# Attention followed by a feed-forward block on one Trainium2 core: Pool's arithmetic moved to DVE and ACT, and the two heads of a pair handled together

## The chip, the cores and the metric

The kernel runs on one core of a Trainium2 chip. A core has a matrix engine (PE, TensorE), a vector engine (DVE), a scalar engine for activations (ACT), a general engine (Pool, GpSimd) and a sync engine (SP) that here issues nearly all DMA transfers. Each has its own list of instructions, which in the traces of this case start in the order in which the program emits them (a copy on ACT at 411.43 us below, for one, starts behind three conversions emitted before it), and waits on the others by semaphores; that order matters more in this case than any single duration.

The metric is the time of one execution in microseconds (us). The kernel before scatters nonetheless, from 1007.5 to 1022.8 us over the chips used, so each kernel is compared with runs of the kernel before on the same chip in the same rounds. A ratio below is the mean time of one kernel's runs over that of the other's of the same rounds, so it is not quite the ratio of the medians that stand beside it; the brackets are its 95% interval.

## The reference, cut to what matters

```python
# attention: q, k, v of (4, 8, 768, 64); proj of (64, 6)
q_bits = (q @ proj > 0);  k_bits = (k @ proj > 0)        # 6 hash bits a row
mask   = q_bucket[..., :, None] == k_bucket[..., None, :]
scores = where(mask, q @ k.T / 8, -1e9)
attn   = exp(scores - max) / (sum + 1e-9)
x      = (attn @ v)  -> (3072, 512)
# feed-forward: w_in (512, 2048), w_out (2048, 512)
return relu(x @ w_in) ** 2 @ w_out
```

The arguments that `setup_inputs` makes for the weights are 64-bit floats (a 32-bit array times a NumPy double), so the kernel has to turn their bits into 32-bit floats itself.

## The kernel before

There are 32 heads, handled two at a time: 16 head pairs, `pr`, one head in each half of the 128 partitions. Each pair is cut into six key blocks (`SB` = 6), so there are 96 steps. A step computes scores of a key block (PE, to the tiles `st`), their exponentials (ACT, `e`), their running sum (DVE, `total`), and, two steps later, the product with the values (PE, `xo`). The masking is done by six hash bits (`bits`): they come from `near` and `far`, which PE computes from transposed inputs `feat`, which DVE transposes for the next pair at key blocks 2 (q) and 3 (k):

```python
PREPARE = ((), (), ((features, 0),), ((features, 1), (hash_bits, 0)), ((hash_bits, 1),), ())

def score(pr, kt):                      # before: one tile and one exponential per head
    ...                                 # matmuls into st[h, c]
    for c, (lo, hi) in enumerate(CUTS):         # columns 0:512 and 512:768
        for h in range(2):
            nc.scalar.activation(
                out=weights[pr, kt, h][:, lo:hi], in_=st[h, c][:, 0:hi - lo],
                func=ACTF.Exp, scale=scale,
            )
```

Between these, two 128x512 pieces of the weights per pair are converted from 64-bit to 32-bit floats: split into exponent and fraction bits on DVE (`part_weight`), the exponent clamped on Pool, and the fraction made a number on ACT; some steps later `round_weight` adds the low bits on DVE and multiplies by the power on Pool:

```python
def part_weight(i):                     # before
    nc.vector.tensor_scalar(out=power, in0=high, ...)     # exponent bits
    nc.vector.tensor_scalar(out=top, in0=high, ...)       # fraction bits
    nc.gpsimd.tensor_scalar(out=power, ..., op0=ALU.min, op1=ALU.max)
    nc.gpsimd.tensor_scalar(out=power, ..., op0=ALU.add, op1=ALU.mult)
    nc.scalar.activation(out=one, in_=top, func=ACTF.Copy, scale=2.0**-23, bias=1.0)

def round_weight(i):
    ...                                                   # two vector instructions
    nc.gpsimd.tensor_tensor(out=pieces[i][3], in0=one, in1=power.bitcast(FP32), op=ALU.mult)
```

The feed-forward stage multiplies by Strassen-like blocks (`product`), which need sums of blocks of its operands. Those of `w_in` (`sums_in`, eight groups of four additions) and of the first part of `x` (`sums_x`) are made during attention. `sums_in` writes over a block of `w_in`, so a copy of that block is stored to DRAM first (`kept_in`), and the first group has to wait until the store has read it:

```python
for u in range(len(steps) + 1):         # the order in which everything is emitted
    add_up(*steps[u - 1]); score(*steps[u])
    ...                                 # spread (reciprocals), PREPARE, attend, sum_up, normalize
    for f, i in w_steps.get(u, ()):     # the weight work of this step, and sums_in
        f(i)
    if u == W_IN:
        nc.sync.dma_start(out=kept_in, in_=w_in[:, 0:2, HF:DFF])
```

## Time and profile before

| | before |
|---|---|
| median of the first three runs | 1016.07 us (1013.56 to 1016.36) |
| span of the profiled run | 1018.9 us |
| one head pair, mean of 13 | 25.66 us |
| first feed-forward matmul | 424.92 us |
| a fixed point in the feed-forward stage (a group of its matmuls) to the end | 474.80 to 1018.90, 544.10 us |

The page's chain of work that ended last, by engine, and the group of the additions (line, engine, operation, output<-input, count | busy us, mean ns | idle before it and its cause) say the same thing from two sides:

```profile
PE 72%; DVE 13%; issue 7%; ACT 5%; DMA 1%; SPq 0%; ACTq 0%; DVEq 0%
L345 DVE TENSOR_TENSOR total<-total,e 128x768 f32<-128x768 f32 x128 | 145.6, 1180 | 3.0 <-ACT e L332 3.0
```

DVE carries 13% of the chain, far more than a helper of a PE-bound kernel should, and its additions take 1180 ns on average. The view of waits from 50 to 410 us (engine, tile and line, what it waited for: us in total, times, longest) sums what PE loses:

```profile
PE st L323 <- ACT e L332: 15.1, 14, 1.4
PE near L284 <- DVE feat L272: 14.4, 15, 3.0
PE near L284 <- ACT e L332: 12.7, 12, 1.3
```

About 42 us of waits in 14 pairs, three a pair.

### The profile page before, as it was taken

How to read it: one execution, taken by the hardware profiler on the slowest of the kernel's cores; microseconds unless marked ns; L12 is line 12 of the kernel's file. 1: busy time of each engine (PE TensorE's matmuls, PEld its weight loads, DVE VectorE, ACT ScalarE, POOL GpSimd, SP SyncE). 2: the span in 40 equal slices, each digit the busy share in tenths (PEclk: the TensorE clock that was granted, in tenths of full speed). 3: DMA queues.
4: the chain of work that ended last, by engine and by line, in shares of the span. 5: the costliest groups of instructions: out<-in, count | busy, mean ns of one | idle time of the engine just before them, and what ended most of it. 6: DMA issues, size and time to landing. Idle time of an engine off the chain costs nothing.

```text
span 1018.9 us, 13495 instructions
## 1 busy us (share of the span) xinstructions
PE 950.0 (93%) x5038; PEld 660.2 (65%) x5038; DVE 613.6 (60%) x1069; ACT 345.6 (34%) x817; POOL 218.0 (21%) x182
## 2 busy tenths in 40 slices
PE   6988989898888889999999999999999999999897
PEld 3333333333333333588888888888888888888786
DVE  1788888888988888998028604840583068106600
ACT  4655555555554555322013102310231032013200
POOL 1233424335776454590000000000000000000000
PEclk9999999999999999999999999999999999999999
DMA  7344444445533522101012202210221021100000
GB/s 165 90 100 113 104 108 105 108 102 148 136 86 92 139 70 85 37 0 43 21 52 67 69 21 68 63 57 21 83 63 52 21 88 58 52 21 1 1 21 23
DMA packets 121159, 70.14 MB, mean 69 GB/s; under 512 B 99328, under 2 KB 104448, under 8 KB 121088
## 3 DMA queue, kind: packets, MB, share of 16 engines
q1 hardware_dynamic: 121024, 69.22, 24.9%
q8 instruction: 41, 0.67, 0.3%
q14 instruction: 30, 0.25, 0.1%
q0 software_dynamic: 64, 0.00, 0.0%
HBM read 54.53 MB, written 14.68 MB: 68 GB/s over the span
## 4 chain that ended last, share of the span: by engine, by line
PE 72%; DVE 13%; issue 7%; ACT 5%; DMA 1%; SPq 0%; ACTq 0%; DVEq 0%
PE acc L554 54%; PE st L323 7%; PE xo L355 6%; ACT bits L290 3%; ACT e L332 3%; PE near L284 2%; DVE power L135 2%; DVE total L345 2%; DVE one L164 2%; DVE one L139 2%; DVE power L160 1%; DVE feat L272 1%; PE tot L372 1%; DVE g L645 1%; DVE h L644 1%
## 5 line engine op out<-in xcount | busy, mean ns | idle before, releaser
L332 ACT ACTIVATE e<-st 128x256 f32<-128x256 f32 (+1 forms) x384 | 157.0, 494 | 120.7 <-PE st L323 92.3
L554 PE MATMUL acc<-x,w_in 128*128 128x256 f32 x768 | 174.7, 379 | 0.0
L554 PE MATMUL acc<-w_out,g 128*128 128x256 f32 x768 | 170.0, 381 | 0.0
L554 PEld LDWEIGHTS acc<-w_out,g 128*128 128x128 f32 x768 | 146.9, 191 | 20.3
L554 PEld LDWEIGHTS acc<-x,w_in 128*128 128x128 f32 x768 | 145.8, 190 | 19.9
L323 PE MATMUL st<-feat,feat 64*128 64x512 f32 (+1 forms) x768 | 156.2, 492 | 0.0
L345 DVE TENSOR_TENSOR total<-total,e 128x768 f32<-128x768 f32 x128 | 145.6, 1180 | 3.0 <-ACT e L332 3.0
L355 PE MATMUL xo<-e,v_nat 128*64 128x512 f32 (+1 forms) x768 | 146.4, 501 | 0.8 <-ACT e L332 0.8
L554 PE MATMUL acc<-t_x,s_in 128*128 128x256 f32 x576 | 132.3, 379 | 2.7 <-ACT one L561 2.7
L554 PE MATMUL acc<-t_out,gs 128*128 128x256 f32 x576 | 126.3, 379 | 0.0
L554 PEld LDWEIGHTS acc<-t_x,s_in 128*128 128x128 f32 x576 | 109.2, 190 | 18.3 <-POOL w_out L431 1.9
L554 PEld LDWEIGHTS acc<-t_out,gs 128*128 128x128 f32 x576 | 109.4, 190 | 14.9
L355 PEld LDWEIGHTS xo<-e,v_nat 128*64 128x64 f32 x768 | 47.4, 137 | 92.2 <-issue 89.9
L677 DVE TENSOR_TENSOR o<-acc,two 128x256 f32<-128x256 f32 x12 | 5.1, 425 | 155.9 <-PE acc L554 155.9
L323 PEld LDWEIGHTS st<-feat,feat 64*128 64x128 f32 x768 | 69.3, 191 | 39.6 <-issue 37.5
L323 PE MATMUL st<-bits,bits 64*128 64x256 bf16 (+1 forms) x384 | 72.1, 330 | 21.1 <-ACT e L332 16.4
L645 DVE SCALAR_TENSOR_TENSOR g<-h 128x256 f32<-128x256 f32 x192 | 82.4, 450 | 5.0
L323 PEld LDWEIGHTS <-bits 64*128 64x128 bf16 x384 | 21.8, 94 | 82.0 <-issue 71.8
L561 ACT COPY two<-acc 128x256 f32<-128x256 f32 x60 | 22.4, 373 | 143.3 <-PE acc L554 143.3
L147 POOL TENSOR_SCALAR power<-power 128x512 uint32<-128x512 uint32 x32 | 54.2, 1694 | 2.6
L167 POOL TENSOR_TENSOR w_in<-one,power 128x512 f32<-128x512 f32 x16 | 34.1, 2130 | 83.3 <-DVE one L164 83.3
L284 PE MATMUL near<-feat,projs 64*64 64x384 f32 x120 | 26.5, 517 | 27.2 <-DVE feat L272 14.4
(90 smaller groups left out, 801.4 us busy)
## 6 DMA issues: line engine op xcount, KB each, us to landing
raw<-in_moe_w_in_dram SPq DMA_DIRECT2D x16, 512.0 KB, 4.3
raw<-in_moe_w_out_dram SPq DMA_DIRECT2D x16, 512.0 KB, 3.9
v_nat<-in_v_dram SPq DMA_DIRECT2D x16, 384.0 KB, 4.8
x_all<-x_t SPq DMA_DIRECT2D x16, 384.0 KB, 2.3
x<-x_all SPq DMA_DIRECT2D x6, 1024.0 KB, 5.3
out_dram<-o SPq DMA_DIRECT2D x24, 256.0 KB, 2.0
raw_qk<-in_k_dram SPq DMA_DIRECT2D x16, 384.0 KB, 3.2
raw_qk<-in_q_dram SPq DMA_DIRECT2D x16, 384.0 KB, 3.1
```

Source lines behind the costliest of these rows:

```text
L135: nc.vector.tensor_scalar(out=power, in0=high, scalar1=20, scalar2=0x7FF, op0=ALU.logical_shift_right, op1=ALU.bitwise_and,)
L147: nc.gpsimd.tensor_scalar(out=power, in0=power, scalar1=-896.0, scalar2=2.0**23, op0=ALU.add, op1=ALU.mult,)
L167: nc.gpsimd.tensor_tensor(out=pieces[i][3], in0=one, in1=power.bitcast(FP32), op=ALU.mult)
L284: nc.tensor.matmul(out=hp[at:at + D, 0:HS], lhsT=projs[rows], rhs=feat[pr, w][rows, c * HS:(c + 1) * HS], start=True, stop=True,)
L290: nc.scalar.activation(out=out, in_=in_, func=ACTF.Sign, scale=HUGE, bias=lifts[at])
L323: nc.tensor.matmul(out=st[h, c][:, 0:hi - lo], lhsT=src[pr, 1][rows, key], rhs=src[pr, 0][rows, lo:hi], start=first, stop=not first,)
L332: nc.scalar.activation(out=weights[pr, kt, h][:, lo:hi], in_=st[h, c][:, 0:hi - lo], func=ACTF.Exp, scale=scale,)
L345: nc.vector.tensor_tensor(out=totals[pr, h], in0=in0, in1=weights[pr, kt, h][:, 0:S], op=ALU.add)
L355: nc.tensor.matmul(out=xo[h * D:(h + 1) * D, lo:hi], lhsT=nat[pr, "v_nat"][:, h, kt * D:(kt + 1) * D], rhs=weights[pr, kt, h][:, lo:hi], s ...
L554: nc.tensor.matmul(out=acc[to], lhsT=a(i), rhs=b(i), start=first and i == 0, stop=last and i == n - 1, skip_group_check=True,)
L561: nc.scalar.copy(out=t, in_=acc[of])
L645: nc.vector.scalar_tensor_tensor(out=out, in0=h, scalar=0.0, in1=h, op0=ALU.max, op1=ALU.mult)
```

## The change

The intent: instructions of Pool slow those of DVE that run beside them (the numbers are in the prediction), so take all arithmetic off Pool while attention runs. The exponent's clamp becomes a Relu with an offset, written to 8 bits, whose range is meant to take the place of the upper limit; the final multiply and the block sums go to DVE. To make room, the exponentials and additions of both heads are merged (one tile `e` of 2 x 768 columns), and the last key block is not added by DVE: PE adds it with eight more matmuls against ones. The split of a weight piece moves from key block 4 to key blocks 5 (even pieces) and 0 of the next pair (odd ones). Cut to its core:

```diff
-        nc.gpsimd.tensor_scalar(... op0=ALU.min, op1=ALU.max)
-        nc.gpsimd.tensor_scalar(... op0=ALU.add, op1=ALU.mult)
+        nc.scalar.activation(out=small, in_=power, func=ACTF.Relu, bias=excess)     # uint8
+        nc.scalar.activation(out=power, in_=small, func=ACTF.Copy, scale=2.0**23)
         nc.scalar.activation(out=one, in_=top, func=ACTF.Copy, scale=2.0**-23, bias=1.0)
 ...
-        nc.gpsimd.tensor_tensor(
+        nc.vector.tensor_tensor(
             out=pieces[i][3], in0=one, in1=power.bitcast(FP32), op=ALU.mult
 ...
-        for c, (lo, hi) in enumerate(CUTS):
-            for h in range(2):
-                nc.scalar.activation(out=weights[pr, kt, h][:, lo:hi], in_=st[h, c]...)
+        for st, (lo, hi) in zip(sts, CUTS):
+            nc.scalar.activation(out=e[:, :, lo:hi], in_=st[:, :, 0:hi - lo], ...)
 ...
     def add_up(pr, kt):
+        if kt == 0 or kt == SB - 1:
+            return
 ...                                             # one addition for both heads
+        for src in (totals[pr], weights[pr, SB - 1]):        # sum_up, on PE
 ...
-        u = i // 2 * SB
-        for n, f in ((i % 2, load_weight), (4, part_weight), (SB + 1 + i % 2, round_weight)):
+        u = i // 2 * SB + i % 2
+        for n, f in ((-3, load_weight), (SB - 1, part_weight), (SB + 1, round_weight)):
 ...
-        w_steps.setdefault(W_IN + 4 * r + 1, []).append((sums_in, r))       # on Pool
+        w_steps.setdefault(W_IN + r * (SB - 1) + 1, []).append((sums_in, r)) # on DVE
```

## The prediction

> **What bounds the kernel now.** I read the page's header and slices first, then busy time by stage, then the idle gaps of PE, then one pair of heads on every engine.
>
> ```profile
> PE 950.0 (93%) x5038; PEld 660.2 (65%) x5038; DVE 613.6 (60%) x1069; ACT 345.6 (34%) x817; POOL 218.0 (21%) x182
> PE   6988989898888889999999999999999999999897
> DVE  1788888888988888998028604840583068106600
> POOL 1233424335776454590000000000000000000000
> ```
>
> Pool works only in the first 18 slices, up to about 460 us. Those are attention and the first part of the feed-forward stage, where PE has holes and DVE is nearly full. After that PE is solid. Busy time by stage (us: stretch and length, PE, PEld, DVE, ACT, POOL, then clock and DMA) puts sizes on it:
>
> ```profile
> 51.30:152.75 101.45, 89.15 (x585) 35.84 (x585) 85.01 (x109) 57.75 (x128) 37.19 (x24) 1.00 0.43 106
> 474.80:1018.90 544.10, 535.59 (x2475) 470.54 (x2474) 224.22 (x541) 97.67 (x262) 0.00 (x0) 1.00 0.14 45
> ```
>
> From 474.8 us on nothing that the change touches can matter: PE is the limit and its matmuls are unchanged. The attention stage lasts to 424.9 us (the first feed-forward matmul starts at 424.92). In the first row, exactly four head pairs, PE idles 12.3 us, 3.1 us a pair. The timeline of PE for one of them (start, length, what, idle before and releaser):
>
> ```profile
> 152.75 0.54 PE L284 MATMUL near<-feat,projs 64*64 64x384 f32 x2 [1.31 <-DVE feat L272]
> 157.72 0.54 PE L284 MATMUL near<-feat,projs 64*64 64x384 f32 x2 [0.93 <-ACT e L332]
> 164.12 0.86 PE L323 MATMUL st<-bits,bits 64*128 64x512 bf16 x2 [0.92 <-ACT e L332]
> ```
>
> Three waits a pair. The first two are hash matmuls waiting for a transpose that DVE makes late. For the second the view names ACT, but the k transpose ended at 157.57 (156.60 + 0.97) and the exponential is no input of this matmul, so I put it down to DVE. The third is ACT: exponentials stood behind a weight conversion, which stood behind DVE. Why DVE is late shows where its timeline is laid beside Pool's:
>
> ```profile
> 153.79 2.89 DVE L345 TENSOR_TENSOR total<-total,e 128x768 f32<-128x768 f32 x2
> 153.95 1.92 POOL L167 TENSOR_TENSOR w_in<-one,power 128x512 f32<-128x512 f32 x1 [2.96 <-DVE one L164]
> 157.50 1.78 DVE L345 TENSOR_TENSOR total<-total,e 128x768 f32<-128x768 f32 x2
> 162.96 0.63 ACT L150 ACTIVATE one<-one 128x512 f32<-128x512 uint32 x1 [0.74 <-DVE one L139]
> 163.50 1.61 ACT L332 ACTIVATE e<-st 128x512 f32<-128x512 f32 x4
> ```
>
> The same two additions take 1.78 us alone and 2.89 us beside a Pool multiply. The last two rows are the third wait: these exponentials read scores finished at 161.69 and start at 163.50. First feature matmul of pair 1 to that of pair 14 is 51.32 to 384.96 us, 333.64 / 13 = 25.66 us a pair.
>
> **What the Trainium skill says.** "SBUF — State Buffer", section "Who interferes with whom": a DVE instruction with two SBUF inputs contends with a GpSimd instruction that reads SBUF, and the later one waits. The trace agrees: 2.89 against 1.78 us. "VectorE: DVE Perf Modes", section "The perf-mode tier table (the rule you actually need)": fp32 tensor_tensor runs in 1x mode. Agreed: 0.89 us for 768 columns is above one per cycle at 0.96 GHz (0.80 us), so merging two additions saves almost nothing but the second's fixed cost. "ScalarE: Activation LUTs", section "What ACT_TABLE_LOAD costs": an ACTIVATE takes 186 ns + 0.833 ns a column, a pointer operand adds about 93 ns, and neighbours overlap by about 93 ns. The trace: 593 and 395 ns for 512 and 256 columns, where the formula gives 613 and 399. I use it for shapes that the trace lacks. The same page, section "Table sets: the hidden batching unit", puts relu in the set of exp, and the changed kernel as built has one table load, as before, so Relu costs no switching.
>
> **The change part by part.**
> PE per pair. From the timeline: score step 1.72 (159.97 to 161.69), attend 1.445, one hash group 0.80, totals 0.78 for eight records, reciprocal matmul 0.33. Before, without waits: 6 x 1.72 + 6 x 1.445 + 2 x 0.80 + 0.78 + 0.33 = 21.7 us. The last key block adds eight records, 0.78 us: 22.5 us is the new floor, on the path.
>
> DVE per pair. Ten additions at 1.18 us (page: 1180 ns) become four merged ones, estimate 2 x 0.80 + 0.09 = 1.69 us each: 11.8 down to 6.8 us. Two weight multiplies come over, about 0.69 each (the 128x512 tensor_tensor of the feed-forward stage takes 692 ns): +1.4. The bit operations lose their inflation (means 743, 835, 691 and 556 ns against about 0.60, 0.60, 0.42 and 0.42): two pieces a pair, about -1.6. In sum DVE goes from 21.3 us a pair (85.01 / 4) to about 16. Late transposes depend on order, not sums. In the built stream each transpose stands behind one weight rounding and one addition. Setting 0 at the pair's first score matmul, PE ends the previous pair's last attend at 8.21. DVE: normalize to 9.27, rounding 1.9 with its multiply now, addition 1.65, q transpose ready at about 13.8; then rounding, addition and k transpose: 18.3. PE with no other wait wants them at 13.1 and, after that first delay, at 17.8. So DVE alone would still cost 0.8 + 0.5 = 1.3 us.
>
> ACT per pair. A step's exponentials go from 1.64 to (estimate by the formula) 1.04 - 0.09 + 0.61 = 1.56 us. Each piece adds a Relu with pointer bias (0.70) and a Copy (0.6). ACT ends near 16 us of 23.8, no bound, but in the built stream the second piece's three conversions now stand in front of the exponentials of key block 1, and they wait for two DVE bit operations placed behind the totals' reciprocal. Chain: totals end on PE 4.72, DVE flip to reciprocals 1.4 (168.54 to 169.95) and the first bit operation to 6.58, Relu 6.66 to 7.36, Copy to 8.04, Copy, exponential of 1024 columns 8.49 to 9.53, then PE's next score. PE wants it at 8.21: a new wait of 1.3 us. It comes ahead of the two transpose waits, and moves PE to 14.4 and 18.4 there, after both transposes are ready. So one wait of 1.3 us replaces three of 3.1 (plus slow restarts), and the period is 22.5 + 1.3 = 23.8 us.
>
> Sum. 25.66 - 23.8 = 1.86 us a pair; pair 0 has no predecessor and pair 15 no successor, so I count 14.5 pairs: -27. Weight sums and the first x sums move from Pool to DVE. Eight groups of four at 0.34 to 0.42 us, 1.5 us each; three of them, and the 2.7 us of x sums, stand before a transpose or the normalize: estimate 1.5 + 1.0 + 0.5 + 2.0 = +5. The end of attention (last scores at 415.80, feed-forward at 424.92: 9.1 us with waits of 0.76 and 0.33 for the last exponentials and addition) should take 2.9 + 1.45 + 1.55 + 1.4 + 0.3 = 7.6: -1.5. In the first feed-forward chunk DVE needs 7.8 us a block beside Pool (452.25 to 460.05 on PE) where PE needs 6.04; without Pool 4.2 + 1.5 for w_out's sums = 5.7, so two waits of 1.18 and 1.52 vanish: -2.7. Total -27 + 5 - 1.5 - 2.7 = -26: 1016.1 - 26 = 990 us.
>
> **The rivals.** (1) *All waits go, PE floor:* 16 more pairs' worth of 1.3 us, about 970. For it: DVE falls to two thirds busy. Against: the order of the streams, in which either DVE or ACT is late by 1.3 us. (2) *ACT becomes the limit of each pair:* if conversions to and from 8 bits are twice as slow, or ACT pays for waiting on itself, the new wait grows to 2.5 to 3 us and nothing is left of attention's gain: 1005 to 1015. For it: ACT waits ended PE's idle time already in every pair. Against: the trace's own conversion from uint32 takes 631 ns, as the formula says. (3) *The coarser buffer costs:* both heads' scores must now finish before one exponential, and PE gets both banks back at once. For it: the third wait is of this kind. Against: both heads' matmuls run side by side and end together, and exponentials usually start idle (0.85 and 1.48 us before). At most 0.2 us a step where ACT is late, about 993. (4) *Loads:* weights are fetched three steps earlier through the same three buffers, so the sync queue blocks on a DVE rounding ahead of q and k loads. Those have over a step sequence of slack (about 20 us against 4.3 to land): nothing.
>
> **Range and chances.** The mechanism gives 990; the size of the new ACT wait is the weak term, +-0.5 us a pair is +-8 us. Range 980 to 1001. Under 995.7 is faster by over 2%: 0.78; within 2%: 0.21; slower: 0.01.
>
> **What would show it.** Right: merged additions near 1.7 us throughout; POOL empty after the start; feed-forward starting near 400 us; hash matmuls mostly without idle before them; one wait of about 1.3 us a pair on `st`, released by ACT, at key block 2; 535.6 us of PE after the first chunk, unchanged. Wrong: additions still near 2.3 us (Pool was not what slowed them), hash matmuls still waiting for `feat`, conversions well over 0.75 us, or a second ACT wait in each pair.

## The result, and the profile after

The changed kernel took 1004.65 us (1000.85 to 1005.03, four runs) against 1016.22 us for the kernel before in the same rounds (1013.56 to 1018.57): ratio 0.9879 [0.9844, 0.9913], faster by 1.2% and inside the 2% that count as the same. The prediction was 990 us with a range of 980 to 1001, so it missed.

The page's header and slices of the changed kernel:

```profile
PE 954.4 (95%) x5166; PEld 661.2 (66%) x5166; DVE 552.3 (55%) x1070; ACT 370.5 (37%) x689; POOL 3.3 (0%) x18
...
PE   6999999998889999899999999999999999999897
...
POOL 1000000000000000000000000000000000000000
...
PE 63%; DVE 3%; ACT 1%; DMA 0%; issue 0%; SPq 0%; DVEq 0%; ACTq 0%
...
L343 DVE TENSOR_TENSOR total<-total,e 128x1536 f32<-128x1536 f32 x48 | 83.6, 1742 | 0.6 <-ACT e L330 0.4
```

Pool is empty, DVE's share of the chain fell from 13% to 3%, and an addition for both heads takes 1742 ns where the two of before took 2 x 1180. So far this is what was predicted. PE's digits are 9 in slices 2 to 9, and fall to 8 in slices 10 to 12 and 17: this is new. The slices are 25 us wide, so these stretches are about 226 to 301 and 401 to 426 us.

Within a steady pair, PE's timeline shows what stands before each of its waiting points (start, length, what, and in brackets the idle time before and its releaser):

```profile
163.20 0.39 PE L325 MATMUL st<-bits,bits 64*128 64x512 bf16 x2 [1.08 <-ACT e L330]
...
168.09 0.54 PE L285 MATMUL near<-feat,projs 64*64 64x384 f32 x2
...
172.28 0.54 PE L285 MATMUL near<-feat,projs 64*64 64x384 f32 x2
...
186.94 0.39 PE L325 MATMUL st<-bits,bits 64*128 64x512 bf16 x2 [1.08 <-ACT e L330]
```

One wait of 1.08 us on ACT, and no bracket on either hash matmul: three waits became one. The period is 186.94 - 163.20 = 23.74 us, the prediction's 23.8. The wait itself has the predicted cause. ACT's timeline just before it:

```profile
160.34 0.72 ACT L147 ACTIVATE small<-power,excess 128x512 uint8<-128x512 uint32 x1 [3.31 <-DVE power L137]
...
162.15 1.49 ACT L330 ACTIVATE e<-st 128x1024 f32<-128x1024 f32 x2
```

ACT sat idle for 3.31 us until DVE delivered the bits of the odd piece, then had three conversions to do (the Relu, and two Copies of 0.63 and 0.61 us on the lines left out) before the exponentials for which PE was waiting.

So the steady pair is right, and the loss is elsewhere. The view of waits between 50 and 400 us finds it:

```profile
PE st L325 <- ACT e L330: 15.0, 15, 1.1
...
PE near L285 <- DVE feat L273: 5.8, 5, 2.7
...
DVE w_in L425 <- DMA kept_in<-w_in: 5.5, 1, 5.5
```

The first line is the steady wait, in 13 of its 15 times at full length. The others are few and long, and one of them is DVE's own, for a DMA. The timeline of PE puts times on them, and shows a second cost and the start of the feed-forward stage:

```profile
231.50 1.51 PE L371 MATMUL tot<-total,ones 128*32 128x384 f32 x8 [3.07 <-DVE total L343]
...
296.27 0.90 PE L285 MATMUL near<-feat,projs 64*64 64x384 f32 x2 [2.71 <-DVE feat L273]
...
407.02 1.97 PE L554 MATMUL acc<-x,w_in 128*128 128x256 f32 x8
...
411.84 4.54 PE L554 MATMUL acc<-t_x,s_in 128*128 128x256 f32 x12 [2.85 <-ACT one L561]
...
419.67 2.75 PE L554 MATMUL acc<-t_x,s_in 128*128 128x256 f32 x12
```

Each long wait is followed by slow matmuls: the totals' eight records take 1.51 us where they take 0.85 elsewhere, two hash records take 0.90 us where they take 0.54 elsewhere, and twelve records of the feed-forward stage take 4.54 us where they take 2.75 eight microseconds later. Busy time in windows (stretch, length, busy us and count for PE, PE weight loads, DVE, ACT, Pool; then the granted clock, DMA share and GB/s) ties it to the clock:

```profile
160.00:180.00 20.00, 18.78 (x126) 7.58 (x124) 15.91 (x19) 15.23 (x23) 0.00 (x0) 1.00 0.54 133
220.00:240.00 20.00, 15.94 (x102) 6.06 (x96) 9.96 (x19) 10.43 (x17) 0.00 (x0) 0.91 0.36 116
...
400.00:420.00 20.00, 15.77 (x80) 10.50 (x79) 12.64 (x29) 6.76 (x14) 0.00 (x0) 0.91 0.05 21
...
458.48:1002.60 544.12, 535.81 (x2475) 470.70 (x2474) 225.08 (x544) 97.64 (x262) 0.00 (x0) 0.99 0.14 45
```

In a normal stretch the clock is 1.00; in these two with a long wait, and in the one around 296 us, its mean is 0.91 over 20 us. The last row is the part of the feed-forward stage that the prediction called untouched: 544.12 us against 544.10 before.

Shorter windows show what the mean hides. The first two of these rows are of the changed kernel. PE is idle for 2.92 of 3.41 us (the wait before 231.50), and then the clock is 0.50 for 3.41 us:

```profile
227.93:231.34 3.41, 0.49 (x6) 0.04 (x2) 1.99 (x2) 0.00 (x0) 0.00 (x0) 1.00 0.02 7
231.34:234.75 3.41, 2.86 (x18) 0.76 (x20) 1.18 (x4) 2.90 (x5) 0.00 (x0) 0.50 0.00 0
...
928.72:932.13 3.41, 2.28 (x11) 1.67 (x9) 1.81 (x5) 0.84 (x3) 0.00 (x0) 1.00 0.01 2
932.13:935.54 3.41, 1.59 (x9) 1.44 (x10) 2.33 (x9) 0.00 (x0) 0.00 (x0) 1.00 0.02 5
```

The last two rows are of `a1_sums`, an experiment below. There a wait of 2.95 us falls across two such windows, and neither is followed by a slow one. In each trace the starts of the slow stretches lie whole multiples of 3.413 us apart, to 0.003 us; in that of the changed kernel 231.34, 296.19, 412.24 and 948.14 are 19, 34 and 157 of them apart. Cut into windows on that grid, the 14 kept traces (from 16 us to 6 us before the end, slow windows themselves left out, counted from the clock records) have 31 windows in which PE is idle for more than 2.02 us. All 31 are followed by a slow one, none of those with less than 1.97 us idle is, and two of the four between are. So in these traces it is not the length of a wait that decides but how much of it falls into one window; and a slow stretch costs up to 1.7 us, half its length.

**Where the time went.** The two profiled spans differ by 16.3 us. Of this, PE is done with the last scores at 399.86 instead of 415.80 (-15.9). From there to the first feed-forward matmul it takes 7.16 instead of 9.12 (-2.0). From that matmul to the end it takes 595.6 instead of 594.0 (+1.6). The prediction had -22 (-27 + 5), -1.5 and -2.7 for these.

### The profile page after: what moved, and what is told of

The parts are those of the page before. It is cut to its first block, busy times and chain, and to the rows that moved or that the text cites. A ratio compares the mean times of both kernels' runs of the same rounds, so it can differ in the third digit from the quotient of the medians. Undisturbed runs are those within 1.5% of the kernel's fastest.

```text
span 1002.6 us, 12942 instructions
## 1 busy us (share of the span) xinstructions
PE 954.4 (95%) x5166; PEld 661.2 (66%) x5166; DVE 552.3 (55%) x1070; ACT 370.5 (37%) x689; POOL 3.3 (0%) x18
## 4 chain that ended last, share of the span: by engine, by line
PE 63%; DVE 3%; ACT 1%; DMA 0%; issue 0%; SPq 0%; DVEq 0%; ACTq 0%
PE acc L554 58%; PE xo L353 2%; PE st L325 2%; DVE total L343 1%; PE tot L371 1%; DVE feat L273 0%; DVE x_t L408 0%; DMA q_nat<-in_q_dram 0%; DVE one L163 0%; DVE power L159 0%; PE near L285 0%; ACT small L147 0%; ACT power L148 0%; DVE flip L377 0%; DVE g L645 0%
## 5 line engine op out<-in xcount | busy, mean ns | idle before, releaser
L330 ACT ACTIVATE e<-st 128x1024 f32<-128x1024 f32 x192 | 144.9, 806 | 75.8 <-PE st L325 75.8
L325 PE MATMUL st<-feat,feat 64*128 64x512 f32 (+1 forms) x768 | 152.8, 489 | 0.0
L343 DVE TENSOR_TENSOR total<-total,e 128x1536 f32<-128x1536 f32 x48 | 83.6, 1742 | 0.6 <-ACT e L330 0.4
L325 PE MATMUL st<-bits,bits 64*128 64x256 bf16 (+1 forms) x384 | 64.5, 330 | 19.6 <-ACT e L330 16.7
L645 DVE SCALAR_TENSOR_TENSOR g<-h 128x256 f32<-128x256 f32 x192 | 77.3, 423 | 4.9
L644 DVE TENSOR_TENSOR h<-acc,two 128x256 f32<-128x256 f32 x48 | 20.4, 425 | 54.2 <-PE acc L554 54.2
L377 DVE STREAM_TRANSPOSE flip<-tot 128x384 f32<-128x384 f32 x16 | 9.3, 583 | 69.7 <-PE tot L371 69.7
L561 ACT COPY one<-acc 128x256 f32<-128x256 f32 x60 | 22.3, 372 | 64.8 <-PE acc L554 64.8
```

The lines of the kernel that those rows point to most:

```text
L325: nc.tensor.matmul(out=st[:, h, 0:hi - lo], lhsT=src[pr, 1][rows, key], rhs=src[pr, 0][rows, lo:hi], start=first, stop=not first,)
L330: nc.scalar.activation(out=e[:, :, lo:hi], in_=st[:, :, 0:hi - lo], func=ACTF.Exp, scale=scale)
L343: nc.vector.tensor_tensor(out=totals[pr], in0=in0, in1=weights[pr, kt][:, :, 0:S], op=ALU.add)
L377: nc.vector.transpose(out=flip, in_=tot[:, 0:HS])
L561: nc.scalar.copy(out=t, in_=acc[of])
L644: nc.vector.tensor_tensor(out=h, in0=one, in1=two, op=ALU.add)
```

## The experiments

The theory to test: the steady pair is worth what was predicted, and two faults of order took it back, namely where the block sums stand in DVE's list, and where the last weight piece stands in DVE's and ACT's. The rivals: the merged tiles cost something that shows nowhere as one wait; ACT's conversions or the eight PE records of the last key block are the true price; or the order of the weight work, and not the relief of Pool, is what earns the gain. Twelve kernels ran on two chips, in three groups; all gave correct results.

### The changed kernel again, beside its repairs

`a0_after` is the changed kernel unedited, as the reference point of its group.

> The changed kernel itself again, on the same chip as the next three, as their reference. My theory: 1000 to 1005 us, with the three long PE waits of its first profile (about 3.1, 2.7 and 2.9 us, in pairs 8 and 11 and at the start of the feed-forward stage), each followed by about 3 us of matmuls at a lower clock. Rival (the long waits were an accident of that one execution): they are missing in this profile and the time is near 990.

Measured: 1003.86 us against 1019.23 of before (ratio 0.9842 [0.9819, 0.9864]). The result of the first comparison holds; on this chip the kernel before is some 3 us slower, so the gain looks larger. The three long waits are there again, 2.63, 2.71 and 2.84 us, so they were no accident of one execution.

### Block sums where DVE has slack

`a1_sums` moves only the eight groups of sums of `w_in` to later steps, at key blocks 4 and 5, where no transpose for PE is pending, the first one six steps later than in the changed kernel; and the sums of `x` one step earlier.

```diff
-        w_steps.setdefault(W_IN + r * (SB - 1) + 1, []).append((sums_in, r))
+        w_steps.setdefault((58, 59, 71, 77, 83, 89, 94, 95)[r], []).append((sums_in, r))
...
-            if u == X_0 + SB:
+            if u == X_0 + SB - 1:
                 sums_x(0)
```

> Changed kernel with the w_in sums and the first x sums in steps where DVE is idle anyway (key blocks 4 and 5, the first one six steps later). My theory: pairs 8 to 12 lost 11.8 us against the steady 23.74 us a pair to these sums (the wait for the kept_in store, x sums and w_in sums ahead of a transpose, and the low clock after waits near 3 us); all pairs should now take 23.7 us, so 9 to 12 us less than a0_after, 992 to 995. Rival 1 (DVE simply has more to do since Pool is idle, wherever the sums stand): within 3 us of a0_after. Rival 2 (loads are late): waits remain in pairs 8 to 12 with a DMA as releaser.

Measured: 989.91 us, ratio 0.9714 [0.9692, 0.9735]: 14.0 us below the changed kernel of the same group, with the same instructions. The place of the sums was the larger fault. The wait before the feed-forward stage's twelve records stays, 2.84 us with 4.54 us after it, as it should where only the sums moved.

### The last weight piece one step earlier

`a2_last` only keeps the split of the last piece from falling behind the last normalize:

```diff
         for n, f in ((-3, load_weight), (SB - 1, part_weight), (SB + 1, round_weight)):
-            w_steps.setdefault(max(u + n, 0), []).append((f, i))
+            at = max(u + n, 0)
+            if f is part_weight:
+                at = min(at, len(steps) - 1)
+            w_steps.setdefault(at, []).append((f, i))
```

> Changed kernel with the last weight piece split one step earlier, so that its three ACT conversions no longer stand between the last attend and the first copy of the feed-forward stage. My theory: the 2.85 us wait of PE for that copy goes, and with it about 1.8 us of slow clock: 4 to 5 us less than a0_after. Rival (DVE's backlog of weight rounding and w_out sums holds the first block anyway): the wait stays or moves to the next block, under 1.5 us gained.

Measured: 999.37 us, ratio 0.9803 [0.9783, 0.9824], that is 4.5 us below the changed kernel. The trace shows why the split mattered. In the changed kernel ACT's list read

```profile
409.62 0.72 ACT L147 ACTIVATE small<-power,excess 128x512 uint8<-128x512 uint32 x1 [6.83 <-DVE power L137]
...
411.43 0.35 ACT L561 COPY one<-acc 128x256 f32<-128x256 f32 x1
```

so the copy that frees the first accumulator stood behind three conversions, which stood 6.83 us waiting for DVE. The wait of 2.85 us and the 1.8 us of slow matmuls after it (4.54 less 2.75) make 4.6 us, and 4.5 came back.

### Both repairs

> Both edits. My theory: they add up, 13 to 16 us less than a0_after, so 988 to 991 us, which is what the prediction said, and feed-forward starts near 395 us; every pair has one PE wait of 1.1 us for ACT at key block 2 and no other. Rival (they share one cause, the slow clock): less than 10 us together.

Measured: 986.78 us, ratio 0.968 [0.966, 0.9701], 17.1 us below the changed kernel; within the prediction's range, and 3 us under its number. Its span is 985.0 us. The repaired stretch on PE's timeline, and the start of the feed-forward stage:

```profile
233.39 0.39 PE L325 MATMUL st<-bits,bits 64*128 64x512 bf16 x2 [1.08 <-ACT e L330]
...
280.87 0.39 PE L325 MATMUL st<-bits,bits 64*128 64x512 bf16 x2 [1.08 <-ACT e L330]
...
393.99 0.40 PE L395 MATMUL tot<-both,picks 128*128 128x24 f32 x2 [1.39 <-DVE both L385]
```

Two pairs with block sums among them take 280.87 - 233.39 = 47.48 us, 23.74 each, and the view of waits has 16 waits on ACT of at most 1.1 us and no other in the steady pairs. The sums on DVE, placed well, cost nothing; the +5 us that the prediction gave them is not a price of the work.

### Each part of the change undone

Three kernels take back one part of the changed kernel each, without the repairs. They ran on another chip than the first group, so they are judged by the steady period in their traces (23.74 us for the changed kernel), which neither fault touches.

`b1_lastdve` adds the last key block on DVE again:

```diff
-        if kt == 0 or kt == SB - 1:
+        if kt == 0:
             return
...
-        for src in (totals[pr], weights[pr, SB - 1]):
+        for src in (totals[pr],):
```

> Changed kernel with one part undone: the last key block is added on DVE again and PE sums only the totals. My theory: PE has 0.76 us less to do in each pair, on the path, and the chain that ends in the one ACT wait of a pair starts earlier by the same; DVE is idle 4.7 us before the flip, so its fifth addition (1.75 us) costs nothing. Steady pairs 23.0 us instead of 23.74, ratio to before near 0.972. Rival (the addition is late for the sums, which is what the change was made for): PE waits for total before the sums, steady pairs 23.7 us or longer.

Measured: 995.66 us, ratio 0.982 [0.9785, 0.9855]. Two neighbouring pairs on PE's timeline:

```profile
158.32 0.39 PE L325 MATMUL st<-bits,bits 64*128 64x512 bf16 x2 [1.08 <-ACT e L330]
...
181.42 0.39 PE L325 MATMUL st<-bits,bits 64*128 64x512 bf16 x2 [1.08 <-ACT e L330]
```

The period is 23.10 us with the same wait of 1.08: the fifth addition on DVE is free in a steady pair, and giving it to PE costs 0.64 us a pair, nearly the 0.78 that the prediction put on the path. This part of the change loses time. The ratio missed the expected 0.972 all the same: the one wait at the block sums, 3.07 us in the changed kernel, is 5.02 us here.

`b2_heads` takes the merging back: a score tile, an exponential and an addition for each head, as before.

```diff
-        return ps_s.tile([P, 2, 512], FP32, name=f"st{c}")
+        return [ps_s.tile([P, 512], FP32, name=f"st{h}{c}") for h in range(2)]
...                                          # and exponentials, additions per head
```

> Changed kernel with one part undone: a tile, an exponential and an addition for each head. My theory: merging the heads is worth nothing by itself, since exponentials start idle and two additions of 0.89 us are as long as one of 1.75: steady pairs within 0.3 us of 23.74, ratio to before 0.980 to 0.989. Rival (fewer, larger instructions carry the gain): steady pairs over 24.3 us. Other rival (the coarse buffer costs): under 23.2 us.

Measured: 1006.4 us, ratio 0.9924 [0.9884, 0.9964], and a steady period of 23.87 us, 0.13 longer than merged. The ACT wait is shorter there, 0.65 us, but its first records then take 0.86 instead of 0.39 us (presumably because one head's bank is free before the other's, which was not tested), and a transpose is late again:

```profile
173.03 0.54 PE L286 MATMUL near<-feat,projs 64*64 64x384 f32 x2 [0.25 <-DVE feat L274]
```

So the coarser buffer does no harm on balance; merging is worth a little. The ratio lies just outside the 0.980 to 0.989 expected.

`b3_clamp` puts the two clamping instructions on Pool again, and takes Relu and Copy off ACT; the multiplies and sums stay on DVE.

```diff
-        nc.scalar.activation(out=small, in_=power, func=ACTF.Relu, bias=excess)
-        nc.scalar.activation(out=power, in_=small, func=ACTF.Copy, scale=2.0**23)
+        nc.gpsimd.tensor_scalar(... op0=ALU.min, op1=ALU.max)
+        nc.gpsimd.tensor_scalar(... op0=ALU.add, op1=ALU.mult)
```

> Changed kernel with one part undone: the two clamp operations of each weight piece on Pool again, everything else off Pool. My theory: ACT has two conversions less in front of the exponentials of key block 1, so the 1.1 us wait of a pair shrinks to 0.0 to 0.3; Pool's two operations a piece slow only what DVE does in their 2 to 4 us (flip, bit operations), and the transposes stay in time: steady pairs 22.6 to 23.3 us, ratio to before 0.965 to 0.977. Rival (any arithmetic on Pool brings back late transposes): hash matmuls wait for feat again and pairs take 24 us or more.

Measured: 1002.44 us, ratio 0.9884 [0.9844, 0.9924]. What I expected of the period was wrong: it did not shrink but stayed at 23.74 us. PE's timeline shows why:

```profile
166.99 0.54 PE L288 MATMUL near<-feat,projs 64*64 64x384 f32 x2 [0.51 <-DVE feat L276]
171.54 0.54 PE L288 MATMUL near<-feat,projs 64*64 64x384 f32 x2 [0.51 <-DVE feat L276]
```

The wait on ACT is gone and two waits on DVE's transposes took its place, 0.51 us each; the next pair's first one is at 190.73, 23.74 us on. The prediction had said so: without the ACT wait, DVE alone would cost 0.8 + 0.5 us, because each transpose stands behind a rounding and an addition. It costs 1.0. Two limits of nearly the same size lie on top of each other, and removing one shows the other. The clamps on Pool took 0.72 and 0.62 us in such a pair of that trace and no DVE work grew beside them.

### Removing both limits by order alone

`c2_rounds` has both repairs and reorders the weight work. The DVE half of both pieces' split comes at key block 5; the ACT half is a function of its own, `scale_weight`, so that it meets finished bits (the odd piece's a step later); and the roundings come at key block 3 of the next pair, after the k transpose. No instruction is added or dropped; one more buffer is needed for the raw weights.

```diff
-        raw = p_w.tile([P, PIECE, 2], U32, name="raw", bufs=3)
+        raw = p_w.tile([P, PIECE, 2], U32, name="raw", bufs=4)
...
+    def scale_weight(i):                    # Relu, Copy, Copy on ACT
...
-        for n, f in ((-3, load_weight), (SB - 1, part_weight), (SB + 1, round_weight)):
+        c = i % 2
+        for n, f in (
+            (-3, load_weight), (SB - 1 - c, part_weight), (SB - 1, scale_weight),
+            (SB + 3 - c, round_weight),
+        ):
```

> Both edits of a3_both, and the weight pieces spread differently: both DVE bit splits at key block 5, the ACT conversions of the second piece one step after its split, both roundings after the k transpose, one more buffer for loads. My theory: the only wait left in a steady pair, 1.1 us for ACT at key block 2, is due to conversions waiting for a split behind the flip; with it gone and no rounding ahead of the transposes, pairs take PE's own 22.5 to 22.7 us: 16 to 20 us under a3_both, ratio to before near 0.950, about 967 to 971 us. Rival (the prediction's own claim, that DVE alone would still cost 1.3 us a pair): only holds if the roundings stay ahead of the transposes, so not here; if pairs still take 23.5 us or more, another chain bounds them.

Measured: 966.95 us against 1015.87 of before, ratio 0.9535 [0.9501, 0.957]. All that PE waits for in the whole of this trace is

```profile
PE tp L269 <- DMA q_nat<-in_q_dram: 5.4, 1, 5.4
PE st L331 <- DVE bits L304: 3.5, 1, 3.5
PE tp L617 <- DVE top L611: 2.9, 1, 2.9
PE tot L401 <- DVE both L391: 1.4, 1, 1.4
PE st L331 <- ACT e L336: 0.6, 1, 0.6
```

which is the start of the program, one wait at the end of attention and one late in the feed-forward stage. No steady pair waits at all. Four pairs, from 82.72 to 172.24 us, take 89.52 us: 22.38 a pair, the floor of 22.5 that the prediction worked out from PE alone.

### Is it only the order?

`d1_order` puts this to the kernel before: Pool keeps all its work, and only the roundings move behind the k transpose (with a fourth raw buffer).

```diff
-        for n, f in ((i % 2, load_weight), (4, part_weight), (SB + 1 + i % 2, round_weight)):
+        for n, f in ((i % 2, load_weight), (4, part_weight), (SB + 3, round_weight)):
```

> The kernel before with its Pool arithmetic untouched; only the weight roundings are moved behind the k transpose (key block 3), with a fourth load buffer. It asks whether Pool or the order made the transposes late. My theory: the order. Both waits for feat (2.2 us a pair) go although Pool still slows additions to 2.9 us; the ACT wait at the next pair's first score (1.3 us with its restart) stays or grows, since DVE stays near full: pairs 23.2 to 24.4 us instead of 25.66, ratio to before 0.97 to 0.985. Rival (Pool contention is the cause and order only moves it): pairs over 25.2 us, ratio over 0.992.

Measured: 1020.19 us against 1018.81, ratio 1.0008 [0.9987, 1.003]. No gain in time; the forecast fell. Both waits for transposes did vanish, but the wait for ACT grew, and two additions beside a Pool multiply still take 2.88 us. The view of waits from 50 to 400 us, and busy time in the same stretch, first of `d1_order` and then of the kernel before:

```profile
PE st L323 <- ACT e L332: 34.2, 14, 5.1
...
50.00:400.00 350.00, 313.72 (x1984) 125.76 (x1982) 302.36 (x367) 194.16 (x436) 148.42 (x120) 0.96 0.44 107
...
50.00:400.00 350.00, 305.36 (x1984) 122.23 (x1982) 298.13 (x369) 198.26 (x440) 169.13 (x119) 1.00 0.42 109
```

14 waits of 34.2 us in all, 2.4 us each, in place of three short waits of 3 us a pair, 42 in all. So PE waits 8 us less, but its 1984 matmuls take 8.4 us more, at a mean clock of 0.96 instead of 1.00: a long wait fills a window of the clock where three short ones do not. The seven pairs that met a slow stretch take 25.8 to 30.3 us, the seven that met none 24.0 to 25.6, against 25.4 for an undisturbed pair before. Two things thus stand against order alone: while DVE's list is nearly full, moving a piece of it makes another piece late, and the one long wait that results costs clock as well. Order pays in full only once there is slack.

### Is an empty Pool needed?

`c4_poolmul` is `c2_rounds` with the final multiply of each piece on Pool again.

```diff
-        nc.vector.tensor_tensor(
+        nc.gpsimd.tensor_tensor(
             out=pieces[i][3], in0=one, in1=power.bitcast(FP32), op=ALU.mult
```

> The kernel of c2_rounds with the last multiply of each weight piece on Pool again, as before the change. My theory: in that order contention hits only work with slack (a rounding and the addition after it, about +1.1 us a pair against 1.4 us of DVE work saved), so pairs stay at PE's 22.4 us and the time within 0.4% of c2_rounds (ratio to before 0.950 to 0.957): taking all arithmetic off Pool is not what pays. Rival (Pool contention must go): pairs over 22.8 us, with waits for feat or total.

Measured: 966.74 us against 1018.81, ratio 0.9487 [0.9468, 0.9506]. The period is again 22.38 us, and over the same 89.52 us PE is again busy throughout. The contention is still there, in the DVE rounding that meets the multiply (1.76 us for one that takes 0.68 alone) and in the multiplies on Pool, 17.47 us for eight in that window, 2.2 us each:

```profile
160.29 1.76 DVE L169 SCALAR_TENSOR_TENSOR one<-raw,one 128x512 f32<-128x512 uint32 x1
```

It costs nothing because nothing on PE's path stands behind it. So the conflict between the two engines is real, and yet a wholly empty Pool is not what the best order needs. Whether that order could also bear the clamps and the block sums on Pool was not run.

### The last key block on DVE, with the rest repaired

`c3_all` is `c2_rounds` with the fifth addition on DVE, the `w_in` sums spread evenly, (60, 66, 72, 78, 84, 90, 94, 95), and the sums of `x` three steps from the end of attention.

> The kernel of c2_rounds with the last key block added on DVE again and the w_in and x sums in steps that leave DVE room before the sums. In the profile of c2_rounds DVE is idle 3.9 us before the flip and PE spends 0.76 us a pair on the second half of the sums. My theory: pairs 21.6 to 21.8 us, 10 to 12 us under c2_rounds (ratio near 0.942). Rival (DVE has then under 1 us of slack and the addition comes late): PE waits for total before the sums in many pairs, gain under 5 us.

Measured: 965.0 us, ratio 0.9467 [0.9445, 0.949], only 1.7 us under `c4_poolmul` of the same rounds, whose runs overlap with these. The steady period is what was expected, 21.73 us (150.30 to 172.03 on DVE's normalize). But I had put the sums of `x` in the last pair before its last additions, where the last two groups of `w_in` sums and two bit splits stand too:

```profile
366.42 1.50 PE L377 MATMUL tot<-total,ones 128*32 128x384 f32 x8 [5.31 <-DVE total L349]
```

The shorter period should earn 0.65 x 15 = 10 us. The wait of 5.31 us and the slow matmuls behind it (1.50 here instead of 0.85, and 3.76 instead of 1.97 for the first eight of the feed-forward stage) gave 7.8 back. It is the fault of the changed kernel again, made by me: with the fifth addition back on DVE, the last additions are on the path to the end of the stage, and anything ahead of them in DVE's list is too. A version with these sums placed elsewhere was not run.

### The wait late in the feed-forward stage

Both kernels have a wait near the end, where a check of the largest inputs (`guard`) lets PE transpose a maximum that DVE has only just begun. In the changed kernel:

```profile
946.82 0.38 PE L604 MATMUL tp<-ident,top 128*1 128x128 f32 x2 [2.95 <-DVE top L598]
947.04 8.76 PE L554 MATMUL acc<-w_out,g 128*128 128x256 f32 x32
```

In `a1_sums` the same wait of 2.95 us is followed by 7.07 us for the same 32 records. `e1_guard` is `c2_rounds` with the maxima taken three iterations before the transposes:

```diff
+                if i == NCHUNK - 1 and r == 2:
+                    guard_max()
+                if i == NCHUNK - 1 and r == 5:
+                    guard()
...
-            if i == NCHUNK - 1:
-                guard()
```

> The kernel of c2_rounds with the overflow check's maxima taken in the third block of the last chunk and its two transposes three blocks later, so that PE does not wait 2.95 us for them just before the last products. Not part of the change; it measures what a wait near 3 us costs with the slow clock after it. My theory: 3 to 4.7 us under c2_rounds (2.95 for the wait, up to 1.7 for slow matmuls where they followed). Rival (PE would wait elsewhere for the last block): under 1.5 us.

Measured: 962.73 us (961.98 to 962.99), ratio 0.9443 [0.9423, 0.9463]; 4.0 us under `c4_poolmul` of the same rounds, which has the same period (`c2_rounds` itself ran on the other chip) and scattered from 963.39 to 968.29. The wait is absent from the trace. Its removal takes the 2.9 us and, where a slow stretch followed, up to 1.7 us of slow matmuls. It followed in the profiled run of `c2_rounds` and not in that of `c4_poolmul`; for the runs without a profile this is inferred from the scatter, which shrinks to one microsecond. This is the fastest version: it beats the kernel before by 5.6% and the changed one by about 4%.

| kernel | median us | before, same rounds | ratio | steady pair us (before and d1_order: mean) |
|---|---|---|---|---|
| before | 1016.22 | | | 25.66 |
| changed | 1004.65 | 1016.22 | 0.9879 | 23.74 |
| a1_sums | 989.91 | 1019.23 | 0.9714 | 23.74 |
| a3_both | 986.78 | 1019.23 | 0.968 | 23.74 |
| b1_lastdve | 995.66 | 1015.87 | 0.982 | 23.10 |
| b3_clamp | 1002.44 | 1015.87 | 0.9884 | 23.74 |
| c2_rounds | 966.95 | 1015.87 | 0.9535 | 22.38 |
| d1_order | 1020.19 | 1018.81 | 1.0008 | 25.68 |
| c4_poolmul | 966.74 | 1018.81 | 0.9487 | 22.38 |
| c3_all | 965.0 | 1018.81 | 0.9467 | 21.73 |
| e1_guard | 962.73 | 1018.81 | 0.9443 | 22.38 |

## Why the prediction was right or wrong

**The bound and the mechanism: right for the steady pair.** DVE's late work was what held PE up, and Pool slowed it; how much of the gain is owed to Pool alone is not separated, since the change also reorders the weight work and takes an addition off DVE. With the change the pair's three waits became one, of 1.08 us where 1.3 was predicted, in the predicted place and for the predicted reason, and the period is 23.74 where 23.8 was predicted. The merged additions take 1.74 us (estimate 1.69), the Relu 0.72 (0.70), the Copy 0.63 (0.6). DVE is busy 17.1 us a pair (68.52 us over the four pairs from 115.72 to 210.68) where about 16 was worked out, and ACT 15.95 (63.82 / 4; near 16). "Sum. 25.66 - 23.8 = 1.86 us a pair; ... I count 14.5 pairs: -27" came out, with some luck: 25.66 holds the one pair of 28.88 us, which Pool's sums of `x` had held up, so that an undisturbed pair gained 1.7 us and the rest came from that one.

**The floor and the limit behind the limit: right.** `c2_rounds` ran at 22.38 us a pair, and `b3_clamp` showed the DVE limit of 1.0 us under the ACT limit of 1.08.

**The block sums: wrong, the larger miss.** The step that failed is "estimate 1.5 + 1.0 + 0.5 + 2.0 = +5". It took the sums as work that delays PE by its own length at most. Measured, the intervals between the ACT waits at key block 2 from pair to pair are 28.18, 24.22, 25.21, 28.19, 24.67 and then 23.73 us: over 23.74 they carry 4.44 + 0.48 + 1.47 + 4.45 + 0.93 = 11.8 us. Two things were left out. The first is a transfer. DVE's timeline:

```profile
229.35 0.43 DVE L425 TENSOR_TENSOR w_in<-w_in,s_in 128x256 f32<-128x256 f32 x1 [5.47 <-DMA kept_in<-w_in]
```

The first group of sums overwrites a block that is still being stored, and DVE stood 5.47 us until the store, issued by the sync engine at 220.38, had landed some 9 us later. In the kernel before nobody had to wait. There the store was issued at 226.2 and landed 6.9 us later, and Pool, with other work ahead in its list, came to the first group only after it:

```profile
243.10 0.72 POOL L422 TENSOR_TENSOR s_in<-w_in 128x256 f32<-128x256 f32 x1
```

DVE came to that point 3.5 us after the store was issued. An instruction moved to another engine can come earlier than it used to, and meet a dependency that was always long satisfied; its wait then holds up all that stands behind it there: here the additions, and through them PE, 3.07 us. The second is the clock: two slow stretches, from 231.34 and 296.19 us, of up to 1.7 us each. The prediction named slow restarts but put no such cost into this sum. Less these two, 3.07 and 3.4, the 11.8 leaves 5.3 us, close to the +5. `a1_sums` confirms the size: 14.0 us came back when the sums moved (11.8 read in the intervals; in the two traces another 1.7 lie at the guard's wait, whose matmuls ran at full rate in that of `a1_sums`, as its windows above show).

**The first feed-forward block: wrong, the smaller miss.** "so two waits of 1.18 and 1.52 vanish: -2.7" failed; measured was +1.6. Those two waits did vanish. But the prediction followed ACT's list only through a steady pair, and not to its end, where the last odd piece has no next pair to fall in and its split lands behind the last normalize. That made a wait of 2.85 us and 1.8 us of slow clock: -2.7 + 4.6 = +1.9. `a2_last` gave 4.5 back.

**The end of attention: right.** Predicted -1.5, measured -2.0, with the wait for the reciprocals 1.39 as its 1.4.

**The sum.** -26 as predicted, +6.8 for the sums (11.8 less 5), +4.3 for the first block (1.6 less -2.7), -0.5 for the end of attention: -15.4, and the spans differ by -16.3. With both faults repaired the time is 986.8, within the range. What the prediction got wrong was not what the change is worth but that two edges of the schedule went unread.

**The rivals.** The first (all waits go) is not what happened, but the order that makes it happen exists. The second (conversions too slow) is refuted by the durations above. The third (the coarser buffer costs) finds no support in `b2_heads`. The fourth named weight loads as harmless, and they were; the transfer that did harm was a store. The rival that the prediction lacked is a moved instruction that comes too early for what it depends on.

**Open.** The grid of the clock above was read from the traces and not put to a test of its own. It was not tried how much of `c3_all`'s 21.73 us a pair can be had with better placed sums.

## What to carry to other kernels

When work moves to another engine, list for each moved instruction what it depends on and when that is ready, not only how long it takes: on the new engine it may come early enough to wait, and then it holds up everything behind it. Follow the new order through the first and last rounds as well as the steady one. For every wait of PE over 2 us, count that up to 1.7 us of slow matmuls may follow; several short waits are cheaper than one long one of the same sum. Less work on a full engine and a better order need each other: here the reordering of the roundings alone gave nothing, the change as made 1.2%, both together about 5%, and 5.6% with the guard's wait removed.

## What the Trainium skill lacked or had wrong

- "TensorE: Matmul & The Clock Gate", section "🔬 Part 1: The HAM clock gate (the "warmup" mystery)", gives an idle window of about 3.4 us, free-running, after which the matrix engine's clock drops to half. The free-running window agrees: half-clock stretches on a grid of 3.413 us. But the window need not be all idle, and the wait need not be that long: after waits of 2.71, 2.85 and 3.07 us, matmuls ran at 0.90 instead of 0.54, 4.54 instead of 2.75 and 1.51 instead of 0.85 us, and in `d1_order` a wait of 2.16 us (to 60.19) was enough. What the section lacks is the share: here about 2.0 us of idle time in one window of 3.413. That also tells apart the guard's wait of 2.95 us with slow matmuls behind it (8.76 us, changed kernel) and without (7.07, `a1_sums`).
- "SBUF — State Buffer", section "Who interferes with whom": agrees, with 2.88 us for two additions beside a Pool multiply against 1.78 alone. To this the runs add a case in which the conflict costs no time: with slack behind the DVE instruction, an inflation from 0.68 to 1.76 us in `c4_poolmul` left the period unchanged.
- "ScalarE: Activation LUTs", section "What ACT_TABLE_LOAD costs": its formula gives 1040 ns for 1024 columns and 706 for 512 with a pointer operand; measured 1020 and 722. The 8-bit conversions, which I found in none of its examples, took 722 ns into uint8 (with the pointer operand) and 630 ns out of it; a Copy from uint32 of that length took 613.
